# Linear attention followed by a spectral mixing layer: p in own slots, q row by row, and another order of the output chunks

## The chip, the cores and the metric

One core of one Trainium2 chip. The metric is the device time of the whole program in microseconds (us), of the slowest core. The first four runs of the kernel before spread by 0.25% (440.9 to 442.0 us), eleven later ones by 0.6% (440.33 to 442.94). This document uses a second measure that is read from the trace: the **output phase**, from the issue of the first copy `yl<-zst` to the end of the span. Everything that the change touches lies within the phase or just ahead of it; the noise of the 408 us before it does not enter. Each phase below comes from one profiled execution.

## The reference

Attention with a feature map, then a Fourier mixing layer over the sequence, then a residual unit. Only the end matters here:

```python
u = x + y                                  # y: inverse transform of the 64 mixed modes
return (u + np.maximum(u @ w_ch, 0.0))     # [8, 576, 512], float32
```

Each output row is p + max(q, 0), with p = x + y and q = (x + y) @ w_ch. The output is 9.4 MB.

## The kernel before

The weights (two sets of 64 matrices) stream through nine slots for most of the run and are the limit until about 404.6 us. The modes come in eight groups. Seven have been absorbed into x (kept in `xs`) and into x @ w_ch (kept in `xw`) by the time that the last one arrives. The last group gives `yst` (its modes) and `zst` (the same times w_ch). What then remains is, for each of 36 chunks of 128 rows, to add the late modes and to store:

```python
class Last:
    def base(self, which):        # the sum so far: q from xw, p from xs (a matmul that reorders rows)
        ...                       # q: a single PSUM bank per chunk (the program has 4); p: a double bank (2)
    def straight(self, which, only=(0, 1)):
        if self.early:            # batch pair 0, chunks 0 to 7: last modes straight from yst / zst
            ...                   # for each chunk of the pair (row a, chunk n):
            pe.matmul((self.q if which else self.p)[a], lhsT=CM[n // 4][:, n % 4],
                      rhs=(yst, zst)[which], start=False, stop=True)
    def late(self, which):
        if self.early:
            return                # all others: last two groups from yl, 32 rows at a time
        ...
        back((self.q if which else self.p)[a], n, bp, CL, yl, slice(r, r + 32), ...)
    def keep_p(self):             # the first two chunks: p is copied out of PSUM
        if not two_p:
            two_p.append(pb.tile([128, 2, DMODEL], F32, name="rl"))
        self.rl = two_p[0][:, self.items[0][1]]
        act.copy(self.rl, self.p[0])
    def relu(self):               # ScalarE: rl (or rx) = max(q, 0)
        ...                       # self.later: GpSimd adds x to rx, so that p needs no matmul from xs
    def store(self):              # VectorE: of = p + rl; SyncE: DMA to the output
        ...
```

`yl` holds the last two groups in blocks of 32 partitions, which the 32-row matmuls read; it is filled by small DMA copies of `yst` and `zst`:

```python
def put(src, o, dst, copies):     # src is yst or zst of group o
    ...
    if o > 5:
        for s in copies:          # two copies each
            (pool if o == 6 else sp).dma_start(yl[r:r + 16], src)
```

Chunks are handled in pairs, in the order of `seq`; TensorE works on the q of one pair (`ahead`) while the p of another is finished:

```python
for g in range(3, len(seq)):
    s, ts = seq[g], [seq[i] for i in ahead[g - 3:g - 2]]
    ...
    for t in ts: t.base(1); t.straight(1)
    if g > 4: s.base(0)
    for t in ts: t.late(1)
    s.late(0)
    for t in ts: t.relu()
    s.store()
    if g == 7:                    # the first pair that goes through GpSimd runs one place further ahead
        seq[10].base(1); seq[10].late(1); seq[10].relu()
```

Of the kernel before, what the change touches and what calls it, by code (L numbers as in the profile page):

```python
# [10 lines left out]
F32 = mybir.dt.float32  # L11
# [8 lines left out]
DMODEL = 512  # L20
# [23 lines left out]
def kernel(  # L44
# [39 lines left out]
    pw = pw_cm.__enter__()  # L84
# [397 lines left out]
    def chunk(bp, n):  # L482
        if n < 8:
            return xs[:, :, bp, 2 * n:2 * n + 2, :].rearrange("p g h d -> p g (h d)")
        return xs[:, :, bp, 16:18, :].rearrange("p g h d -> p g (h d)")
# [96 lines left out]
    def bank(shape=(128, DMODEL), dt=F32):  # L582
        return pst.tile(list(shape), dt, name="pt", tag="pt")

    def banks(dt=F32):
        return pst2.tile([128, 2, DMODEL * (1 if dt == F32 else 2)], dt, name="pp", tag="pp")

    pb_cm = tc.tile_pool(name="pb", bufs=2)
    pb = pb_cm.__enter__()
# [235 lines left out]
    class Last:  # L825
# [5 lines left out]
            self.first = bp == 0 and n < 2  # L831
            self.later = n == 8 or items[0] in stored

        def base(self, which):
            if self.first:
                if which:
                    if not two_q:
                        two_q.append(banks())
                    self.q = [two_q[0][:, self.items[0][1]]]
                else:  # L840
                    self.p = [bank()]
            elif which:
                self.q = [bank() for _ in self.items]
            else:
                self.pp = banks()
                self.p = [self.pp[:, a] for a in range(2)]
            for a, (bp, n) in enumerate(self.items):
                turned = ident_b if self.later else perm
                if self.later and not which:
                    continue  # L850
                if which:
                    pe.matmul(self.q[a], lhsT=turned, rhs=xw[:, bp, n, :],
                              start=True, stop=False)
                else:
                    pe.matmul(self.p[a].rearrange("p (g e) -> p g e", g=4), lhsT=turned,
                              rhs=chunk(bp, n), start=True, stop=False)
# [15 lines left out]
                              rhs=(yst, zst)[which], start=False, stop=True)  # L872

        def keep_p(self):
            if not two_p:
                two_p.append(pb.tile([128, 2, DMODEL], F32, name="rl"))
            self.rl = two_p[0][:, self.items[0][1]]
            act.copy(self.rl, self.p[0])

        def relu(self):  # L880
# [33 lines left out]
                o.rearrange("p a e -> p (a e)") if w > 1 else o)  # L914

    pairs = [[((bp, n), (bp, n + 1)) for n in (0, 2, 4, 6)] for bp in range(NP)]
    two_q, two_p = [], []
    seq = [Last((0, 0)), Last((0, 1))] + [Last(*x) for x in pairs[0][1:] + pairs[1]]
    seq += [Last(*x) for x in (pairs[2][1], pairs[2][0], pairs[3][0], pairs[2][2], pairs[3][1])]
    seq += [Last((0, 8), (1, 8)), Last(*pairs[3][2]), Last((2, 8), (3, 8)), Last(*pairs[2][3])]  # L920
    seq += [Last((3, 6)), Last((3, 7))]
    H = DMODEL // 2
    while mixq:
        key = mixq.pop(0)
        g, o, i = key[0], key[1] // 2, key[1] % 2
# [61 lines left out]
    seq[1].keep_p()  # L987
    for i in range(2):
        seq[i].straight(1)
    seq[2].straight(0, (1,))  # L990
    seq[2].base(1)
    seq[2].straight(1)
    seq[2].relu()
    seq[0].store()
    seq[1].store()
# [3 lines left out]
    seq[3].base(0)  # L999
    seq[3].straight(0)  # L1000
    seq[3].relu()
    ahead = [4, 5, 6, 7, 8, 9, 12, 11, 14, 13, 16, 15, 17, 18, 19]
    for g in range(3, len(seq)):
        s, ts = seq[g], [seq[i] for i in ahead[g - 3:g - 2]]
        if g == 4:
            s.base(0)
            s.straight(0)
        for t in ts:
            t.base(1)
            t.straight(1)  # L1010
        if g > 4:
            s.base(0)
        for t in ts:
            t.late(1)
        s.late(0)
        for t in ts:
            t.relu()
        s.store()
        if g == 7:
            seq[10].base(1)  # L1020
            seq[10].late(1)
            seq[10].relu()
    pb_cm.__exit__(None, None, None)
    pw_cm.__exit__(None, None, None)

# [28 lines left out]
```

## Time and profile before

| | |
|---|---|
| whole program, median | 441.33 us (441.18 to 442.0), later 441.25 with a fourth run |
| span of the profiled run | 440.0 us |
| first `yl<-zst` copy issued | 408.21 us |
| output phase | 31.75 us |
| last byte of the stores, from that issue | 30.00 us |
| last store tile started on VectorE, from that issue | 26.41 us |

Two rates set this phase: how fast tiles become ready (TensorE, then ScalarE, then VectorE) and how fast 16 transfer engines write them. The best view of the second is the view by stretches, whose last two columns are the mean busy share of the 16 engines and GB/s. (1 - share) x length is the transfer time that a stretch wastes. (This is rough: near 411 us windows of half a microsecond show shares up to 1.27, so a stretch there may waste more than it seems.) Five stretches of the kernel before, cut at 1.2, 5.5, 11, 16 us after the first `yl<-zst` issue and 1.5 us ahead of the last byte:

```profile
409.41:413.71 4.30, 4.30 (x23) 1.77 (x20) 3.41 (x5) 3.15 (x6) 0.00 (x0) 1.00 0.85 220
413.71:419.21 5.50, 5.48 (x32) 1.66 (x32) 4.47 (x4) 4.30 (x9) 0.00 (x0) 1.00 0.85 346
419.21:424.21 5.00, 4.91 (x31) 1.42 (x30) 3.70 (x4) 4.25 (x10) 4.05 (x4) 1.00 0.78 314
424.21:436.71 12.50, 8.55 (x48) 2.40 (x46) 9.70 (x10) 6.44 (x12) 7.31 (x7) 0.93 0.99 393
436.71:438.21 1.50, 0.00 (x0) 0.00 (x0) 0.00 (x0) 0.00 (x0) 0.00 (x0) 0.50 0.70 269
```

Wasted: 0.65 + 0.83 + 1.10 + 0.13 + 0.45 = 3.1 us. The first three are holes, in which no tile was ready. The last is another thing: all data is queued (the last store was issued at 435.33), but the share is 0.70: some of the 16 engines finish sooner than others.

### The profile page before, as it was taken

Reading aid. Unit: us, or ns where it says so; the run is one execution under the profiler, and the core shown is the slowest. Engines: PE = TensorE matmul, PEld = TensorE weight load, DVE = VectorE, ACT = ScalarE, POOL = GpSimd, SP = SyncE. Lnnn points to the kernel's source line nnn. Section 1 sums busy time; section 2 is a strip of 40 time slices with the busy share of each in tenths; the row PEclk is TensorE's granted clock in tenths of the full one; section 3 lists DMA queues with packets and bytes.
Section 4 is the critical chain, followed back from the end, with each engine's and each line's share of the span. In section 5 each row is a group of like instructions: output and inputs, shape, how many; then the busy total and the mean of one; then the engine's idle time right before and its main releaser. Section 6 shows DMA issues by size and latency. Waiting matters only on the chain.

```text
span 440.0 us, 10106 instructions
## 1 busy us (share of the span) xinstructions
PE 326.7 (74%) x4190; PEld 199.7 (45%) x4233; DVE 296.0 (67%) x583; ACT 279.1 (63%) x478; POOL 112.5 (26%) x151
## 2 busy tenths in 40 slices
PE   1676668787678687778787777174679998997993
PEld 0445546555455455455455455051435454333320
DVE  5568787567785777886886878243883334885684
ACT  2788887687896777885875876210644442764782
POOL 6232132132211222221222121121101121582072
PEclk9989988689998799896896999675999999999997
DMA  8999999999999999999999999999999999996787
GB/s 193 210 211 210 237 212 238 231 217 241 235 211 239 221 230 234 237 213 235 228 221 238 210 235 209 236 209 212 212 215 223 220 221 223 206 218 150 238 361 310
DMA packets 51710, 99.55 MB, mean 226 GB/s; under 512 B 2512, under 2 KB 13648, under 8 KB 51664
## 3 DMA queue, kind: packets, MB, share of 16 engines
q0 software_dynamic: 45232, 85.86, 99.6%
q1 hardware_dynamic: 6432, 13.04, 8.5%
q8 instruction: 33, 0.54, 0.4%
q14 instruction: 13, 0.11, 0.1%
HBM read 163.64 MB, written 9.44 MB: 393 GB/s over the span
## 4 chain that ended last, share of the span: by engine, by line
PE 32%; DMA 31%; DVE 15%; ACT 15%; issue 5%; POOL 0%; POOLq 0%; ACTq 0%; DVEq 0%
DMA wt<-in_moe_w_i_dram 14%; PE pt L37 13%; PE one L37 12%; DMA wt<-in_moe_w_r_dram 8%; DMA vn<-in_v_dram 7%; ACT AB L37 6%; PE two L37 6%; DVE m L37 4%; DVE mk L37 4%; ACT AQ L37 3%; DMA qb<-in_q_dram 2%; PE pp L37 2%; ACT XT L37 2%; ACT qT L37 2%; DVE xw L37 1%
## 5 line engine op out<-in xcount | busy, mean ns | idle before, releaser
L37 ACT ACTIVATE AB<-two 128x1024 bf16<-128x1024 f32 x64 | 62.1, 1026 | 12.5 <-DVE mk L37 10.1
L37 ACT ACTIVATE AQ<-two 128x1024 bf16<-128x1024 f32 x64 | 62.7, 1046 | 1.3 <-PE two L37 1.2
L37 ACT CAST xw<-pt 128x512 bf16<-128x512 f32 x50 | 29.3, 587 | 42.3 <-PE pt L37 42.2
L37 DVE TENSOR_TENSOR va<-vn,ee 128x1152 bf16<-128x1152 f32 x32 | 42.0, 1355 | 11.9 <-DMA vn<-in_v_dram 11.9
L37 DVE TENSOR_REDUCE m<-two 128x8 f32<-128x1024 f32 x32 | 39.1, 1223 | 14.9 <-PE two L37 14.6
L37 DVE TENSOR_REDUCE mk<-two 128x8 f32<-128x1024 f32 x32 | 38.9, 1218 | 9.8 <-PE two L37 9.8
L37 POOL DMA_DIRECT2D wt<-in_moe_w_i_dram x28 | 20.9, 748 | 88.0 <-PE pt L37 36.2
L37 POOL DMA_DIRECT2D wt<-in_moe_w_r_dram x30 | 22.5, 749 | 72.3 <-PE one L37 29.3
L37 PE MATMUL pt<-wchb,xT 128*128 128x512 bf16 x127 | 34.7, 385 | 5.7 <-DVE xT L37 4.2
L37 PEld LDWEIGHTS <-xs 128*128 128x128 bf16 x624 | 31.3, 102 | 12.5 <-issue 7.5
L37 PE MATMUL two<-w2blk,qT 128*128 128x256 bf16 x128 | 21.9, 298 | 19.7 <-ACT AB L37 8.8
L37 ACT COPY qT<-one 128x512 bf16<-128x512 bf16 (+1 forms) x32 | 19.2, 641 | 26.4 <-PE one L37 26.2
L37 PE MATMUL one<-wt,XT 128*32 128x512 bf16 x304 | 27.7, 456 | 5.7 <-DMA wt<-in_moe_w_i_dram 4.1
L37 PE MATMUL one<-va,AB 64*128 64x65 bf16 x1024 | 23.1, 200 | 10.9 <-DVE va L37 10.9
L37 PEld LDWEIGHTS <-qT 128*128 128x128 bf16 x144 | 14.4, 102 | 36.7 <-issue 33.3
L37 PE MATMUL two<-mT,minus 96*128 96x512 bf16 x64 | 27.0, 423 | 3.4 <-issue 1.3
L37 DVE COPY xT<-pt 128x512 bf16<-128x512 bf16 x36 | 17.0, 472 | 17.3 <-PE pt L37 17.3
L37 PEld LDWEIGHTS <-AQ 128*128 128x128 bf16 x512 | 24.5, 108 | 8.2 <-issue 4.7
L37 PEld LDWEIGHTS <-XT 128*32 128x32 bf16 x512 | 14.7, 149 | 29.5 <-issue 23.2
L37 PE MATMUL one<-kvz,AQ 128*128 128x65 bf16 x512 | 27.2, 208 | 1.1 <-ACT qT L37 0.8
L37 DVE TENSOR_TENSOR xs<-one,rd 128x384 bf16<-128x384 f32 x48 | 26.8, 557 | 1.6
L37 PEld LDWEIGHTS <-AB 64*128 64x128 bf16 x1024 | 20.7, 101 | 15.0 <-DVE va L37 9.3
(151 smaller groups left out, 700.5 us busy)
## 6 DMA issues: line engine op xcount, KB each, us to landing
wt<-in_moe_w_r_dram POOLq DMA_DIRECT2D x30, 1024.0 KB, 28.6
wt<-in_moe_w_i_dram POOLq DMA_DIRECT2D x28, 1024.0 KB, 29.1
out_dram<-of SPq DMA_DIRECT2D x16, 512.0 KB, 3.7
vn<-in_v_dram POOLq DMA_DIRECT2D x14, 576.0 KB, 25.0
kb<-in_k_dram POOLq DMA_DIRECT2D x16, 288.0 KB, 22.0
qb<-in_q_dram POOLq DMA_DIRECT2D x16, 288.0 KB, 20.5
xs<-in_moe_w_i_dram POOLq DMA_DIRECT2D x2, 1024.0 KB, 24.1
vn<-in_v_dram SPq DMA_DIRECT2D x2, 576.0 KB, 6.7
```

Source lines behind the costliest of these rows:

```text
L37: ins = f(*args, **kwargs)
```

## The change

The intent, as the code shows it: free the buffer that the first two p occupy; finish the first row of the third chunk's q earlier so that its store starts earlier; and move one of the three slow straight pairs at the front to a later place, with another order of running ahead. The core of the diff:

```diff
-        def base(self, which):
+        def base(self, which, only=(0, 1)):      # one row of a pair alone
 ...
         def keep_p(self):
-            if not two_p:
-                two_p.append(pb.tile([128, 2, DMODEL], F32, name="rl"))
-            self.rl = two_p[0][:, self.items[0][1]]
+            self.rl = pw.tile([128, DMODEL], F32, name="rp", tag="wt")
 ...
-    seq = [Last((0, 0)), Last((0, 1))] + [Last(*x) for x in pairs[0][1:] + pairs[1]]
+    seq = [Last((0, 0)), Last((0, 1))] + [Last(*x) for x in pairs[0][1:3] + pairs[1]]
     seq += [Last(*x) for x in (pairs[2][1], pairs[2][0], pairs[3][0], pairs[2][2], pairs[3][1])]
-    seq += [Last((0, 8), (1, 8)), Last(*pairs[3][2]), Last((2, 8), (3, 8)), Last(*pairs[2][3])]
+    seq += [Last((0, 8), (1, 8)), Last(*pairs[0][3]), Last((2, 8), (3, 8))]
+    seq += [Last(*pairs[3][2]), Last(*pairs[2][3])]
 ...
+    for a in range(2):
+        seq[2].base(1, (a,))
+        seq[2].straight(1, (a,))
     seq[2].straight(0, (1,))
-    seq[2].base(1)
-    seq[2].straight(1)
 ...
-    ahead = [4, 5, 6, 7, 8, 9, 12, 11, 14, 13, 16, 15, 17, 18, 19]
+    ahead = [4, 5, 6, 7, 8, 11, 10, 13, 12, 15, 14, 17, 16, 18, 19]
 ...  # base(0) and straight(0) now in one place of the loop
-        if g == 7:
-            seq[10].base(1); seq[10].late(1); seq[10].relu()
+        if g == 6:
+            seq[9].base(1); seq[9].late(1); seq[9].relu()
```

More of the change, by code (lines that the diff above doesn't have):

```diff
@@ L842, in base @@
             elif which:
-                self.q = [bank() for _ in self.items]
+                if 0 in only:
+                    self.q = [bank() for _ in self.items]
             else:
@@ L848, in base @@
                 turned = ident_b if self.later else perm
-                if self.later and not which:
+                if a not in only or self.later and not which:
                     continue
@@ L916 @@
     pairs = [[((bp, n), (bp, n + 1)) for n in (0, 2, 4, 6)] for bp in range(NP)]
-    two_q, two_p = [], []
-    seq = [Last((0, 0)), Last((0, 1))] + [Last(*x) for x in pairs[0][1:] + pairs[1]]
+    two_q = []
+    seq = [Last((0, 0)), Last((0, 1))] + [Last(*x) for x in pairs[0][1:3] + pairs[1]]
     seq += [Last(*x) for x in (pairs[2][1], pairs[2][0], pairs[3][0], pairs[2][2], pairs[3][1])]
-    seq += [Last((0, 8), (1, 8)), Last(*pairs[3][2]), Last((2, 8), (3, 8)), Last(*pairs[2][3])]
+    seq += [Last((0, 8), (1, 8)), Last(*pairs[0][3]), Last((2, 8), (3, 8))]
+    seq += [Last(*pairs[3][2]), Last(*pairs[2][3])]
     seq += [Last((3, 6)), Last((3, 7))]
@@ L1001 @@
     seq[3].relu()
-    ahead = [4, 5, 6, 7, 8, 9, 12, 11, 14, 13, 16, 15, 17, 18, 19]
+    ahead = [4, 5, 6, 7, 8, 11, 10, 13, 12, 15, 14, 17, 16, 18, 19]
     for g in range(3, len(seq)):
         s, ts = seq[g], [seq[i] for i in ahead[g - 3:g - 2]]
-        if g == 4:
-            s.base(0)
-            s.straight(0)
         for t in ts:
@@ L1010 @@
             t.straight(1)
-        if g > 4:
+        if g > 3:
             s.base(0)
+            s.straight(0)
         for t in ts:
@@ L1018 @@
         s.store()
-        if g == 7:
-            seq[10].base(1)
-            seq[10].late(1)
-            seq[10].relu()
+        if g == 6:
+            seq[9].base(1)
+            seq[9].late(1)
+            seq[9].relu()
     pb_cm.__exit__(None, None, None)
```

## The prediction

> **What bounds the kernel now.** I read the page first. The weights occupy the transfer engines until about 404.6 us, and the diff touches nothing before the last weight has been used, so only the output phase counts: 408.2 us to the end, some 32 us of 440. There I read the view by stretches for the transfer rate, then the timelines of VectorE, SyncE and TensorE.
>
> ```profile
> 412.00:412.50 0.50, 0.50 (x4) 0.20 (x2) 0.50 (x2) 0.20 (x1) 0.00 (x0) 1.00 1.07 410
> 413.00:413.50 0.50, 0.50 (x4) 0.16 (x2) 0.30 (x2) 0.38 (x1) 0.00 (x0) 1.00 0.37 147
> 416.00:416.50 0.50, 0.50 (x6) 0.10 (x4) 0.50 (x1) 0.50 (x2) 0.00 (x0) 1.00 1.01 418
> 417.50:418.00 0.50, 0.50 (x6) 0.19 (x6) 0.50 (x1) 0.48 (x1) 0.00 (x0) 1.00 0.00 0
> 422.00:422.50 0.50, 0.50 (x6) 0.10 (x4) 0.50 (x1) 0.50 (x2) 0.21 (x2) 1.00 0.06 25
> 431.50:432.00 0.50, 0.00 (x0) 0.00 (x0) 0.50 (x1) 0.29 (x1) 0.50 (x1) 1.00 0.99 381
> ```
>
> Columns: stretch, length, busy PE, PEld, DVE, ACT, POOL, then clock, DMA share, GB/s. With data to move the stores run at 380 to 420 GB/s; there are holes at about 413.2, 417.4 to 418.0 and 422.0 to 423.0, and none afterwards. So the end is set by 9.4 MB of stores plus these holes, and holes come from late store tiles. These are VectorE's:
>
> ```profile
> 408.90 1.29 DVE L37 SCALAR_TENSOR_TENSOR ofr<-pp,rl 128x512 f32<-128x512 f32 x2 [0.76 <-ACT rl L37]
> 410.89 2.35 DVE L37 TENSOR_TENSOR of<-pp,rl 128x1024 f32<-128x1024 f32 x2 [0.70 <-ACT rl L37]
> 413.44 1.23 DVE L37 TENSOR_TENSOR of<-pp,rl 128x1024 f32<-128x1024 f32 x1 [0.20 <-ACT rl L37]
> 415.57 3.79 DVE L37 TENSOR_TENSOR of<-pp,rl 128x1024 f32<-128x1024 f32 x3 [0.92 <-PE pp L37]
> 420.60 2.52 DVE L37 TENSOR_TENSOR of<-pp,rl 128x1024 f32<-128x1024 f32 x2 [1.23 <-PE pp L37]
> ...
> 432.55 1.22 DVE L37 TENSOR_TENSOR of<-pp,rx 128x1024 f32<-128x1024 f32 x1 [0.49 <-POOL rx L37]
> 433.69 0.68 DVE L37 TENSOR_TENSOR ofr<-pp,rl 128x512 f32<-128x512 f32 x1
> 434.61 0.69 DVE L37 TENSOR_TENSOR ofr<-pp,rl 128x512 f32<-128x512 f32 x1 [0.24 <-issue]
> ```
>
> Its two long waits, 0.92 and 1.23 us, are for TensorE. TensorE is busy without a break to 431.3 us, so it paces the front of the phase. At the back both limits meet: the last tile is ready at 435.30 us, and a half-size store lands some 3.3 us after issue [...].
>
> TensorE's costs, from starts in its timeline: 0.215 us a full matmul; a group of 32-row matmuls (the late modes from yl), two or four together, adds 0.32 before it and 0.32 to the next, 0.43 more than it replaces. A straight pair has eight full matmuls, 8 x 0.215 = 1.72 us; an ordinary pair four and a group, 0.86 + 0.43 = 1.29; a pair whose x goes through GpSimd, 0.86. VectorE needs 1.23 for a pair, a 512 KB store 5.77 MB/11 in 15.0 us = 1.36. The three straight pairs that stand first in the kernel before are the slow ones.
>
> [...]
>
> ```profile
> 408.21 1.19 SPq L37 DMA_DIRECT2D yl<-zst  x2
> DMA to landing us min/median/max: 3.3/3.7/3.8
> 413.71 0.39 PE L37 MATMUL pt<-yl,CL 32*128 32x512 bf16 x2
> ```
>
> (SyncE's timeline, the view of the tile yl, TensorE's timeline.) The second copy is issued at about 408.80, so it lands at about 412.55. The first matmul that reads yl runs at 413.71: 1.1 us of slack today. [...]
>
> **The change, part by part.**
>
> Own slots for p: nothing is removed from the path. p's old tile is one of two rl buffers, which the fourth chunk's relu needs back after 410.19 us; that relu starts at 410.74 for want of TensorE's result. The new tiles take weight slots that are free by then. Worth 0.
>
> Row by row: the order of the build shows the same number of TensorE instructions. The first row of q of the third chunk (a straight pair) is finished after two matmuls instead of four, and the yst matmul of p moves behind. The first relu comes 2 x 0.215 = 0.43 us earlier (409.77 to 409.34), the second ends at 410.42 instead of 410.86 (ScalarE's spacing is 0.49), so the first full store tile starts at 410.46 instead of 410.89; the second, about 411.74 instead of 412.03. Gain: 0.3 to 0.43 on the first two stores.
>
> Order: pair 0/3 (straight) leaves the fifth chunk's place. After the fourth chunk's last matmul (411.24, unchanged), TensorE has two base matmuls (411.45, 411.67) and then wants yl at 411.99, where before came 1.72 us of straight work. But yl lands at 412.55. **A new wait of about 0.6 us on the busiest engine**; without it the order would be free.
>
> I then carried the schedule through by hand with these durations, the engine order of the build, and the buffers (four single banks for q, two double banks for p, two rl). Second yl matmul at 412.62, next pair 412.94, its xs 413.37, group 413.91, tile 0.58 after the group:
>
> | full store tile | before starts | after, worked out |
> |---|---|---|
> | first, second | 410.89, 412.03 | 410.46, 411.74 |
> | third | 413.44 | 414.49 |
> | fourth, fifth | 415.57, 416.85 | 415.78, 417.07 |
> | sixth, seventh | 418.1, 420.60 | 419.56, 420.85 |
> | tenth | 424.5 | 424.86 |
> | twelfth | 427.15 | 427.63 |
> | sixteenth | 432.55 | 433.0 |
> | last half tile | 434.61 | 435.07 |
>
> The q run ahead (first GpSimd pair, 0.86 us of TensorE) now stands one store earlier, so its hole moves from before the seventh tile to before the sixth. At the end the wait for GpSimd (0.49) goes, because its last pair is now one place further ahead; but the straight pair costs TensorE 0.43 more there than the ordinary pair it displaces, and the stall is not recovered, because TensorE, VectorE and the stores all take 1.2 to 1.36 us a pair. Result: the last tile 0.45 us later.
>
> Stores, by the same table: data starts 1.2 us after issue (417.35 to 418.03 ends with the store issued at 416.83). Holes: about 1.3 us before the third store, 1.1 before the sixth. Sum 2.4, against 0.2 + 0.7 + 1.0 = 1.9 now: plus 0.5, with 0.2 won back by the earlier first store (the bytes ahead of it end at 413.1, so not all 0.43 counts). From the sixth store's data at 422.0, eleven full stores and two halves, twelve units of 1.366, end at 438.4 against 438.1: plus 0.3. Both limits say 0.3 to 0.45 us later.
>
> **The rivals.**
> 1. *No stall.* If yl landed by 412.0, the same hand schedule puts the last tile at 434.03 instead of 434.61: a gain of 0.6 us, 440.75. For it: such a reordering is surely meant to fill holes. Against it: 3.3 to 3.8 us to landing, and nothing in the change moves these copies.
> 2. *A fuller recovery.* If the stall is absorbed because TensorE regains slack after the sixth tile, the end is set by the stores alone and the gain of the removed GpSimd wait shows: 440.9 to 441.3. For it: TensorE idles at 418.6, 419.0 and 431.5. Against it: these are waits for banks which the new order has too.
> 3. *Slot waits.* Store tiles share weight slots; one late tile waits for a store only four places back. If stores back up, VectorE waits for landings: plus 0.5 to 1 us, 442.3. For it: landing takes 3.7 to 4 us. Against it: by my table that store lands some 0.7 us before it is needed.
>
> **Range and chances.** The calculation gives 441.33 + 0.4 = 441.7; leaning a little to the first two rivals, 441.5. Hand scheduling is good to some 0.5 us, and three runs spread over 0.8 us, so 440.4 to 442.6. Two per cent is 8.8 us, more than all the holes and waits of this phase: a change of that size is next to impossible.
>
> **What would show it.** Right: TensorE waits 0.4 to 0.7 us for yl just before 412.6 us; first full tile at about 410.46; the third later than 413.44; transfer holes near 416 and 421; no wait for GpSimd at the end; last half tile at about 435. Wrong: no wait at yl, a third tile before 414, or holes that sum to under 1.5 us.

The forecast's sum came to 441.33 + 0.4 = 441.7, leaned to 441.5. What the sum uses of the hardware are measured times of the kernel before: 0.215 us from one full matmul to the next, 0.32 on either side of a group of 32-row matmuls, 1.23 for a pair on VectorE, 1.36 for a 512 KB store (5.77 MB/11 in 15.0 us), 3.3 to 3.8 from issue to landing for the copies that feed `yl`. The last of these is the middle line of the last fence.

## The result, and the profile after

The changed kernel took 442.26 us in the median (441.26 to 442.61, four runs); the kernel before, in the same rounds, 441.25. The ratio is 1.0017, 95% interval 0.9996 to 1.0038: the same within 2%, and the difference is not even clear of zero. The prediction of 441.5, 440.4 to 442.6, holds it.

The profiled runs show more. The changed kernel's span is 440.2 us with the first `yl<-zst` at 407.72: an output phase of 32.52 us instead of 31.75, plus 0.77. The front happened to be 0.5 us shorter in this run.

SyncE's timeline after has the issue from which all is counted (start, length, engine, operation):

```profile
407.72 1.19 SPq L37 DMA_DIRECT2D yl<-zst  x2
```

TensorE's timeline after has the wait that was forecast; the bracket is idle time before the instruction, and what ended it:

```profile
411.49 0.39 PE L37 MATMUL pt<-yl,CL 32*128 32x512 bf16 x1
412.13 0.39 PE L37 MATMUL pt<-yl,CL 32*128 32x512 bf16 x1 [0.25 <-DMA yl<-zst]
```

Before, the two matmuls from yl ran together. Now the second starts 0.64 us after the first. (The bracket gives 0.25 because the first matmul's own 0.39 is not counted as idle.)

VectorE's timeline after:

```profile
409.97 2.52 DVE L37 TENSOR_TENSOR of<-pp,rl 128x1024 f32<-128x1024 f32 x2 [0.26 <-ACT rl L37]
414.00 3.79 DVE L37 TENSOR_TENSOR of<-pp,rl 128x1024 f32<-128x1024 f32 x3 [1.51 <-PE pp L37]
419.02 2.52 DVE L37 TENSOR_TENSOR of<-pp,rl 128x1024 f32<-128x1024 f32 x2 [1.23 <-PE pp L37]
...
430.94 1.21 DVE L37 TENSOR_TENSOR of<-pp,rl 128x1024 f32<-128x1024 f32 x1
432.08 1.21 DVE L37 TENSOR_TENSOR of<-pp,rx 128x1024 f32<-128x1024 f32 x1
433.21 0.68 DVE L37 TENSOR_TENSOR ofr<-pp,rl 128x512 f32<-128x512 f32 x1
434.13 0.69 DVE L37 TENSOR_TENSOR ofr<-pp,rl 128x512 f32<-128x512 f32 x1 [0.24 <-issue]
```

One wait of 1.51 us ahead of the third tile stands where the kernel before had waits of 0.20 and 0.92 ahead of the third and fourth. The wait for GpSimd near the end is gone. The last tile starts at 434.13 - 407.72 = 26.41 us after the issue, to the hundredth where it was. In between they are later: the fifteenth full tile starts at 430.94 - 407.72 = 23.22 us after the issue, before at 22.64. The kernel before then waits 0.49 for GpSimd, the changed one does not, and they are level. **So the last tiles are ready as early as before, and yet the phase is 0.77 us longer.** The same five stretches of the changed kernel say where that went:

```profile
408.92:413.22 4.30, 4.05 (x19) 1.47 (x16) 3.24 (x4) 3.30 (x6) 0.00 (x0) 1.00 0.94 258
413.22:418.72 5.50, 5.39 (x34) 1.56 (x32) 3.67 (x3) 4.24 (x8) 0.43 (x1) 1.00 0.74 302
418.72:423.72 5.00, 5.00 (x35) 1.43 (x32) 4.36 (x4) 4.24 (x8) 4.60 (x5) 1.00 0.77 311
423.72:437.11 13.39, 9.14 (x48) 2.69 (x48) 10.02 (x10) 6.51 (x12) 6.33 (x6) 0.91 0.99 393
437.11:438.61 1.50, 0.00 (x0) 0.00 (x0) 0.00 (x0) 0.00 (x0) 0.00 (x0) 0.50 0.26 100
```

Wasted: 0.26 + 1.43 + 1.15 + 0.13 + 1.11 = 4.1 us, about 0.9 more. (The last byte came 30.89 us after the issue instead of 30.00, plus 0.89; the span shows 0.77 of that.) The holes account for 0.3 (2.84 against 2.57 in the first three stretches: 0.4 won by the earlier first store, 0.6 lost ahead of the third). The larger part, 0.66, is the last stretch: the share is 0.26 instead of 0.70. Most of the 16 engines are done, and a few, or one, still work. The median time from issue to landing of the full stores grew too, as the two pages say, before and after:

```profile
out_dram<-of SPq DMA_DIRECT2D x16, 512.0 KB, 3.7
out_dram<-of SPq DMA_DIRECT2D x16, 512.0 KB, 4.3
```

Why would one lag? The list of DMA queues, asked for 1.3 us windows, shows one packet that is not data: an instruction fetch of 16 KB. The columns are packets, MB and share of the 16 engines' time. Before, from 422.6 to 423.9 us:

```profile
q1 hardware_dynamic: 83, 0.34, 65.1%
q8 instruction: 1, 0.02, 5.7%
```

After, from 423.1 to 424.4 us:

```profile
q1 hardware_dynamic: 139, 0.50, 97.2%
q8 instruction: 1, 0.02, 5.9%
```

5.9% of 16 engines for 1.3 us is one engine for 1.2 us. In both kernels it is the only packet of this size in the phase; it starts 14.44 us after the issue before, and 15.44 after. (Another instruction queue, q14, has two packets of 8 KB, 0.31 us each, in both: at about 12 and 27 us.) Before, the fetch begins in the last hole, which ends at 14.84, and outlasts it by 0.8 us. After, the last hole ends at 13.76, and the whole fetch falls among stores. The page of the kernel before has 33 packets in this queue, 0.54 MB or 16 KB each, and 8423 recorded TensorE instructions (4190 + 4233), which is 255 a packet; that of the changed kernel has 33 and 8466 (4233 + 4233), which is 257. Where the texts below speak of 256 instructions to a fetch, it is an estimate, an average that lies between these two counts; the experiments with doubled transposes test it.

### The profile page after: what moved, and what is told of

The parts are those of the page before. It is cut to its first block, busy times and chain, and to the rows that moved or that the text cites. A ratio compares the mean times of both kernels' runs of the same rounds, so it can differ in the third digit from the quotient of the medians. Undisturbed runs are those within 1.5% of the kernel's fastest.

```text
span 440.2 us, 10147 instructions
## 1 busy us (share of the span) xinstructions
PE 337.2 (77%) x4233; PEld 203.5 (46%) x4233; DVE 296.3 (67%) x583; ACT 279.8 (64%) x478; POOL 112.5 (26%) x151
## 4 chain that ended last, share of the span: by engine, by line
PE 35%; DMA 25%; ACT 17%; DVE 16%; issue 5%; POOL 0%; SPq 0%; ACTq 0%; DVEq 0%; POOLq 0%
PE one L37 14%; DMA wt<-in_moe_w_i_dram 14%; PE pt L37 13%; DMA wt<-in_moe_w_r_dram 8%; ACT AB L37 7%; PE two L37 7%; DVE m L37 5%; DVE mk L37 4%; ACT AQ L37 4%; ACT XT L37 2%; DMA qb<-in_q_dram 2%; PE pp L37 2%; ACT qT L37 1%; DVE xw L37 1%; DVE XT L37 1%
## 5 line engine op out<-in xcount | busy, mean ns | idle before, releaser
L37 PE MATMUL pt<-wchb,xT 128*128 128x512 bf16 x136 | 35.8, 387 | 5.0 <-DVE xT L37 3.8
L37 PE MATMUL two<-qT,w2blk 128*128 128x512 bf16 x64 | 28.0, 438 | 3.6 <-ACT AQ L37 3.5
L37 PEld LDWEIGHTS <-AQ 128*128 128x128 bf16 x512 | 26.6, 114 | 8.7 <-issue 5.4
L37 PE MATMUL one<-kvz,AQ 128*128 128x65 bf16 x512 | 29.2, 216 | 0.9 <-ACT qT L37 0.8
L37 DVE RECIPROCAL rd<-one 128x6 f32<-128x6 f32 x48 | 9.4, 196 | 28.8 <-PE one L37 28.7
L37 PE MATMUL two<-mT,minus 96*128 96x512 bf16 x64 | 28.1, 439 | 0.0
```

What stands on the lines that cost most here:

```text
L37: ins = f(*args, **kwargs)
```

## The experiments

Two theories remained, and a rival to both. *Yl wait*: TensorE's wait for the copies costs the time. *Fetch*: a fetch behind the last hole makes one engine late for good (this rests on my supposition, which no run shows, that every store is spread over all 16 and that those behind the fetch are not moved to another; the packets, after experiment 8, show that "for good" is too strong). *Straight pair*: the slow pair near the end costs it. All kernels passed as correct, the two that are wrong too. "Waste at the end" is (1 - share) x 1.5 us of the last stretch.

**1. The wait for yl taken away (wrong).** The wait was removed by exchanging the data: the fifth chunk's q reads the last group from `zst`, which has been there for microseconds. The result passed as correct all the same, presumably since the term is small.

```diff
+                if which and self is seq[4]:
+                    pe.matmul(self.q[a], lhsT=CL[r:r + 32, n % 4, :], rhs=zst[r:r + 32], ...)
+                    continue
                 back(..., CL, yl, slice(r, r + 32), ...)
```

> Wrong result on purpose: the fifth chunk's late term of q reads the last zst tile, which TensorE has had for 4 us, instead of yl, so the wait for the copies is gone and all else stays. Phase = span minus the issue of the first yl<-zst copy: before 31.75, after 32.52 us. If the yl wait makes the end (the prediction's theory): the two matmuls run together at 3.8 us after that issue, the third store tile starts at 5.6 instead of 6.27, the hole in front of the third store shrinks by 0.6 us, and the phase is 0.4 to 0.7 us shorter (31.8 to 32.1). If the cost is the straight pair at the back (rival), the phase stays within 0.15 of 32.5. If the cost is the 16 KB instruction fetch that occupies one transfer engine for 1.2 us in the middle of the stores, the phase shortens by the hole only, and the last 1.5 us still show about 1 us of idle transfer engines.

Third tile at 5.64 instead of 6.27, phase 32.05 instead of 32.52; ratio to the kernel before 0.999 (0.997 to 1.0011). The wait is worth 0.47 us here, against the straight-pair rival. But the last stretch is still uneven:

```profile
435.67:437.17 1.50, 0.00 (x0) 0.00 (x0) 0.00 (x0) 0.00 (x0) 0.00 (x0) 0.50 0.44 171
```

The stream also breaks off in the middle, between 423.5 and 424.5:

```profile
423.50:424.00 0.50, 0.50 (x7) 0.17 (x4) 0.23 (x2) 0.42 (x1) 0.39 (x1) 1.00 0.48 180
424.00:424.50 0.50, 0.50 (x4) 0.19 (x2) 0.50 (x1) 0.50 (x2) 0.25 (x1) 1.00 0.50 205
```

The store that belongs there was issued by an instruction of 1.05 us, where the median is 0.54, soon after the fetch (at 14.68, 421.43 on this clock); so the fetch may cost this run more than the waste at its end. That waste is 0.84, and the last tile was ready at 25.77, 0.64 earlier than before: the phase is still 0.3 longer than the old kernel's. Something else costs time.

**2. The wait filled with other work.** The right result; base matmuls of two chunks that need no yl go ahead of the first use of yl.

```diff
+        if g == 3:
+            seq[5].base(1)
+            seq[4].base(0)
 ...
         for t in ts:
             t.late(1)
+        if g == 3:
+            seq[4].late(0)
```

> Right result. Base matmuls of the fifth and sixth chunk that need no yl run ahead of the first use of yl. Yl wait theory: TensorE has no gap before the first yl matmul, the third tile starts at 5.7 to 6.1 instead of 6.27, the fourth at about 7.0 instead of 7.54, phase 0.4 to 0.7 us shorter than after's 32.52. Straight-pair theory: no change. Fetch theory: the hole's share only, with the last 1.5 us as uneven as before.

Third tile at 6.17, fourth at 7.49, phase 32.36; ratio 1.0002 (0.9981 to 1.0022). A miss: only 0.16 us of the expected 0.4 to 0.7, less than the 0.22 by which two looks can differ. Both matmuls from yl now run together at 4.63, after the copies; the chunk's two relus follow, and VectorE waits for those instead. TensorE's idle time was filled, but the third tile itself cannot be finished before yl has landed. The last stretch stays uneven, with a share of 0.32.

**3. The old order with the other two parts kept.**

```diff
-    seq = [...] + [Last(*x) for x in pairs[0][1:3] + pairs[1]]
-    ahead = [4, 5, 6, 7, 8, 11, 10, 13, 12, 15, 14, 17, 16, 18, 19]
+    seq = [...] + [Last(*x) for x in pairs[0][1:] + pairs[1]]
+    ahead = [4, 5, 6, 7, 8, 9, 12, 11, 14, 13, 16, 15, 17, 18, 19]
 ...
```

> The changed kernel with the old order of chunks and run-ahead; own slots for p and q row by row stay. Store tiles: the first at 2.25 and the second at 3.55 as in after, from the third on as in before less 0.2 to 0.4. If the order is the loss, the phase is 31.3 to 31.8 us, as before or 0.4 shorter. If slots or rows were the loss, it stays near 32.5. The fetch should fall near 14.4, as in the kernel before, and the last 1.5 us should show about 0.4 us of idle engines.

Phase 31.79, ratio 0.9997 (0.9974 to 1.002). First tiles at 2.25 and 3.54 (before: 2.68 and 3.82), but the third at 5.23 and the later ones as before, where 0.2 to 0.4 less was expected; the last half tile starts 0.43 later. The 0.43 us won on the first store comes back as a longer hole behind it: the second stretch's share falls from 0.85 to 0.77. So q row by row is worth nothing in the old order, and the loss is the order's.

**4. The order alone.** The kernel before with only `seq`, `ahead` and the loop of the changed one.

> The kernel before with the new order of chunks and run-ahead alone (old p tile, old third chunk). If the order is the whole loss: first tiles at 2.68 and 3.82 as before, TensorE waits for yl at about 3.8 to 4.4 as in after, third tile at 6.2 to 6.3, phase 32.4 to 32.7. If q row by row or the slots carried part of the loss: phase nearer to 31.75.

Phase 32.80, ratio 1.0008 (0.9988 to 1.0028): a little longer than expected and 0.28 longer than with all parts. The order carries the whole loss. Whether q row by row recovers a part of it in the new order is not shown: the 0.28 is near the spread of two looks, and the fetch moved too. It falls at 16.01, the latest but one of all, and the waste at the end is 1.35.

**5. The fetch moved into a hole.** 42 transposes far ahead are done twice (the second writes the same again), so by the estimate above every later boundary of 256 instructions comes 84 instructions sooner in the program.

```diff
+    pads = [0] * 42
...
+                if flat and self.g >= 2 and pads:
+                    pads.pop()
+                    pe.transpose(ptr[:, j - lo, :], rows[:, j * 128:(j + 1) * 128], ident_b)
```

> Right result. The changed kernel with 42 transposes done twice some 200 us earlier (84 more TensorE instructions), which moves the boundary of 256 TensorE instructions at which 16 KB are fetched from 15.4 to about 7.4 us after the first zst copy, into the hole in front of the third store. Nothing in the output phase is changed otherwise. Fetch theory: the phase is 0.5 to 0.8 us shorter than after's 32.52, idle engines in the last 1.5 us fall from 1.1 to some 0.4. Yl-wait and straight-pair theories: the phase stays within 0.15 of 32.5; the front may lose up to 1 us from the doubled transposes, so the whole time is judged second.

The fetch moved to 7.91, the phase fell to 31.81, and the share in the last stretch rose to 0.63. About 0.2 of the 0.71 us is luck: yl's second matmul ran at 4.18 instead of 4.41 in this run, and the third tile at 6.05. The whole time was 442.1 us, ratio 1.0016 (0.9995 to 1.0037): in the profiled run the first `yl<-zst` copy was issued at 408.40. In this execution TensorE's granted clock was 0.50 to 0.57 from 405 to 408.5 us, where the changed kernel had 1.00, so `zst` came 3.38 us after `yst` instead of 2.02; that probably is the luck with yl, since no transfer was under way any more when its last copies were issued (DMA share 0.00 from 408.0 to 408.5).

**6. The same in the kernel before, and a control.** The same edit with 8 and with 21 transposes (in group 2 alone).

> The kernel before with 8 transposes done twice far ahead (16 more TensorE instructions), so that the 16 KB instruction fetch moves from 14.4 to about 13.4 us after the first zst copy, wholly into the hole before the seventh store. Store tiles unchanged (last at 26.4). Fetch theory: phase 31.75 falls to 31.2 to 31.5, idle engines in the last 1.5 us from 0.44 to under 0.3. If the fetch does not matter: 31.6 to 31.9 with the same unevenness at the end.

> Control: the kernel before with 21 doubled transposes (42 more instructions), so the fetch falls at about 10.9 us, in a saturated stretch between two holes and not in a hole. Store tiles unchanged. Fetch theory: one engine falls behind by 1.2 us and catches up only by what it can use of the hole at 13 to 14.8 (the other 15 wait there), so the result lies between: phase 31.3 to 31.9; if a lag is never made good, 32.2 to 32.4. If the doubled transposes themselves changed the phase, both paddings would shift it by the same amount.

The fetch went to 13.96 and 11.37, the phases are 31.82 and 31.78 (before: 31.75): ratios 0.9986 (0.9967 to 1.0004) and 1.0001 (0.9977 to 1.0024). My expectation for the first was wrong: nothing was left to gain from this fetch (why, the packets after experiment 8 show). The control shows that this fetch in mid-stream, at 11.37 with the last hole still to come, did no harm either (31.78 against 31.75); that the late engine catches up in that hole is my explanation, not shown. And both show that the doubled transposes do not lengthen the phase.

**7. A candidate: old order, q row by row, 8 doubled transposes.**

> Candidate for the best: old order with q row by row and own slots, and the same 8 doubled transposes. Fetch theory: phase 31.79 falls to 31.2 to 31.5 (the last half tile at 26.4 to 26.8 leaves no more). If the fetch does not matter: 31.7 to 31.9. Whole time 0 to 0.6 us under the kernel before, hard to tell from noise of the front.

Phase 31.80, ratio 0.9998 (0.9974 to 1.0021): no better than the kernel before, for the reasons of 3 and 6.

**8. The converse: the fetch moved behind the last hole in the kernel before.** The same edit with 122 transposes (from the first group on).

> Converse test. The kernel before with 122 transposes doubled far ahead (244 more TensorE instructions), so that the next 256-instruction boundary falls with about 101 TensorE instructions left, at some 15.6 us after the first zst copy: after the last transfer hole (14.84) instead of inside it. Store tiles as before, last at 26.4. Fetch theory as the runs so far have it (a fetch before or in the last hole is made good, one after it is not): phase 32.2 to 32.5 instead of 31.75, idle engines in the last 1.5 us about 1.1 instead of 0.44. If the unevenness comes with the new order and not with the fetch: 31.7 to 31.9.

The fetch fell at 16.36, with all store tiles where they were (last at 26.47). Phase 32.39, plus 0.64; ratio 1.0023 (1.0006 to 1.004), the only interval that excludes 1; as one of thirteen at 95% it would prove little without the trace. The last stretch:

```profile
437.43:438.93 1.50, 0.00 (x0) 0.00 (x0) 0.00 (x0) 0.00 (x0) 0.00 (x0) 0.50 0.23 89
```

A share of 0.23 instead of 0.70, without any change to the output phase's own instructions. The unevenness comes with the fetch, not with the order.

*What the packets add.* The trace does not number the engines, but every store ends with 16 packets of 4 bytes, presumably one on each engine. In the changed kernel, 15 of these come together, within 0.2 us, for the stores after the fetch, and one comes late: for the store that the 15 finish at 16.34 to 16.49 us after the issue it comes at 18.28, then at 19.53, 20.78, 22.03, and so on to 30.88, the last packet of all. In experiment 8 the same begins at 19.39 instead of 17.5 and ends at 30.74. So one engine falls behind at the fetch, by some 1.9 us; why by more than the 1.2 to 1.4 us of the fetch itself stays open. It is not late for good: it takes 1.25 us a store where the others take 1.3 to 1.4, and is 1.2 late at the end. In the kernel before, one engine is 1.1 late just after the last hole (17.26) and about 0.3 at the end (29.86); the very last packet, at 30.00, seems to be another engine's, which ended a store at 27.01 us, at the moment when an 8 KB fetch began. Such a fetch comes at about 27 us in every run, and the kernels of experiments 5 to 7 seem to end in the same way (last bytes at 30.0 to 30.1). This would explain why moving the 16 KB fetch gained nothing in the kernel before; no run moves the 8 KB one, so it is read, not tested.

**9. The fetch moved in the changed kernel, with and without the wait.** 14 doubled transposes, in group 2; the second kernel also has the edit of 1 (wrong).

> The changed kernel with 14 doubled transposes (28 instructions): the fetch moves from 15.4 to about 12.7, ahead of the end of the last hole (13.76); yl and all store tiles as in after (third at 6.27). Fetch theory: phase 31.9 to 32.1 instead of 32.52, idle in the last 1.5 us 0.4 to 0.6 instead of 1.08. Otherwise 32.4 to 32.6.

> Wrong result on purpose: e4 (no wait for yl) and the 14 doubled transposes together, fetch at about 12.1, before the end of that kernel's last hole (13.12). If the two costs are separate and add: 32.05 less 0.3 to 0.5, phase 31.4 to 31.8, idle in the last 1.5 us 0.4 to 0.6. If they are one cost seen twice: 32.0.

The fetches fell at 13.00 and 12.64 (in all six padded runs for which I had named a place, the fetch came 0.3 to 0.8 us after it, so the estimate of 256 instructions holds that far); phases 32.22 and 31.49; ratios 1.0003 (0.9984 to 1.0022) and 0.9996 (0.998 to 1.0012). The last stretch of both has a share of 0.64:

```profile
436.88:438.38 1.50, 0.00 (x0) 0.00 (x0) 0.00 (x0) 0.00 (x0) 0.00 (x0) 0.50 0.64 246
435.77:437.27 1.50, 0.00 (x0) 0.00 (x0) 0.00 (x0) 0.00 (x0) 0.00 (x0) 0.50 0.64 247
```

The first was 0.1 to 0.2 longer than expected: the fetch ran from 13.00 to 14.09 and the hole ended at 13.77, so a part of it fell among stores. In a table of the output phase:

| new order | wait for yl | no wait |
|---|---|---|
| fetch behind the last hole | 32.52 | 32.05 |
| fetch reaching into it | 32.22 | 31.49 |

Alone, the wait costs 0.73 (32.22 - 31.49) and the late fetch 0.56 (32.05 - 31.49); together 1.03. (The 32.05 holds the break in mid-stream of experiment 1.) Without either, the phase is 0.26 us **shorter** than the 31.75 of the kernel before, although the straight pair still stands near the end: that rival falls. The sum is 31.75 - 0.26 + 1.03 = 32.52.

**10. The slots undone.** The changed kernel with p in one `rl` buffer again.

```diff
-            self.rl = pw.tile([128, DMODEL], F32, name="rp", tag="wt")
+            if not two_p:
+                two_p.append(pb.tile([128, 2, DMODEL], F32, name="rl"))
+            self.rl = two_p[0][:, self.items[0][1]]
```

> The changed kernel with p kept in one rl buffer again instead of own slots. All theories: no difference, first tiles at 0.70, 1.31, 2.24, phase 32.3 to 32.7. If the relu of the fourth chunk now waits for the buffer, the second tile starts after 3.6.

First tiles at 0.70, 1.31 and 2.25, second full tile at 3.50, no new wait; phase 32.30, ratio 1.0015 (0.9989 to 1.0041). The own slots do nothing that shows. The 0.22 us to 32.52 with the same store tiles and the same fetch (15.35) shows how far two looks at such a kernel can differ, and how far the table above may be trusted: the two costs stand out of it, but their last digits do not, and neither does the sub-additive part; the gain of 0.26 is about the size of that spread, so it is likely rather than shown.

No version with the right result beat both kernels clear of noise. To have the 0.26 us, if it is real, yl would have to land earlier.

## Why the prediction was right or wrong

**Right.** The first tile was to start 0.43 us earlier: 0.43. TensorE was to wait about 0.6 us for yl: 0.64. The third tile was to start at 414.49, that is 6.28 after the issue: 6.27; the fourth to seventh came within 0.06 us of the table. The slots were to be worth 0: experiment 10. The wait for GpSimd at the end was to go: it did. Holes near 416 and 421 us: they end at 416.4 and 421.5. Holes plus 0.3 net: 2.84 against 2.57. (The sums that the prediction gave, 2.4 and 1.9, are both low: it put the first hole at 0.2 us, while its own line for 413.0 to 413.5 alone wastes 0.3. The difference came out right.) The first rival (no stall) fell on the trace, the third (waits for slots) too: no VectorE line names a landing as what ended a wait. One reading was loose: TensorE is not "busy without a break to 431.3", but idle for 0.11 us at 419, as the second rival itself says.

**Wrong in two steps which the total hides.** "The stall is not recovered", and with it the last tile 0.45 us later: it came at the same 26.41. One term that was mis-sized is "VectorE needs 1.23 for a pair". That is the duration, not the pitch: after a tile that reads rl, one that reads rx (or the reverse, near the end) can start 1.14 us later, as 430.94 to 432.08 shows above. In my table the error is 0.06 at the sixth tile, 0.29 at the tenth, 0.45 at the last. Five such steps of 1.14 after the sixth tile, 0.09 each, sum to 0.45; that VectorE alone set them all is not shown. The last of the delay went where the kernel before waits for GpSimd. The prediction named a fuller recovery as its second rival, with the gain of that wait, and for the last tiles the rival was right; its range, 440.9 to 441.3, was not.

The other is "twelve units of 1.366 end at 438.4", plus 0.3 for the stores. The last byte came 0.89 us later than before (30.89 against 30.00 after the issue). The term takes 16 engines as one. The holes behaved as worked out; what was missing is the engine that is taken for 1.2 us to fetch instructions. In the kernel before that cost was already there, but the fetch began in a hole and the delay was mostly made up by the end, and no line that I quoted could have shown it. In the new order the late hole ends sooner and the fetch comes behind it. Experiment 8 shows this by moving nothing but the fetch; experiment 9 agrees. That the late engine is the very one that fetched is inferred from the moment at which one engine falls behind: the trace does not number the engines.

So the result fell into the range with a cause half right, and in part by luck: the tiles' end was put 0.45 too late and the stores' end 0.6 too early. Of the 0.77 us, the wait that was forecast and the fetch have shares of about the same size, by a table good to some 0.2 us; the gain of the order itself, if it is real, is set off against both.

## What to carry to other kernels

When the end of a program is a stream of stores, ask three things apart: when the tiles are ready, how much of the stream is holes, and how evenly the transfer engines finish; a low DMA share at the very end, with everything issued, was the sign of the third here (0.26 in the last 1.5 us of the changed kernel, 0.70 before). A reordering that fills a hole can lay bare something that was hidden in it: here the last hole ended at 13.76 instead of 14.84, and the fetch at 15.44 fell behind it. And where a change moves the first use of a freshly copied tile forward, compare it with issue plus time to landing (3.3 to 3.8 us for these copies): that sum foretold the wait here to within 0.05 us.
